# Three reorderings in a fused attention and expert kernel: the readers of the global product, the third products of the first slots, and the last unit's readings

## The chip, the core and the metric

One core of a Trainium2 chip runs the whole program. The core has five engines that run their own instruction streams in order and meet at semaphores: TensorE (PE) for matrix products, VectorE (DVE), ScalarE (ACT), GpSimd (POOL) and SyncE (SP), the last two here also issuing most of the DMAs. TensorE writes its results to PSUM, a small memory from which VectorE and ScalarE copy them to the large one, SBUF. The metric is the time of one execution in microseconds, as the device measures it.

## The reference

A block of attention with local and global tokens feeds a layer of eight experts whose gates are balanced by Sinkhorn iterations. Inputs are eight batches of eight heads with 512 local and 32 global tokens of 64 elements, weights for eight experts with 512 inputs and 1024 hidden values.

```python
# attention: global queries see all keys; local ones a band of 32 to each side and the global keys
s_g   = scale * q_g @ concat(k_g, k_l)^T
out_g = softmax(s_g) @ concat(v_g, v_l)
s_l   = concat(scale * q_l @ k_g^T, where(|i-j| <= 32, scale * q_l @ k_l^T, -1e9))
out_l = softmax(s_l) @ concat(v_g, v_l)
x = concat(out_g, out_l)                      # 4352 tokens of 512
# experts
P = exp(x @ w_gate - max)
for _ in range(8):
    P /= P.sum(1) + 1e-9;  P /= P.sum(0) + 1e-9;  P *= N / E      # N = 4352 tokens, E = 8
out = sum_e P[:, e] * (relu(x @ w1[e]) @ w2[e])
```

## The kernel before

The order on every engine is written out by hand: each engine executes its instructions in the order in which the Python code emits them, and the framework adds the semaphore waits. Buffers come from pools: a tile gets a buffer of its tag when that buffer's last reader is done. The pools that matter here are in PSUM: `ps_mm` (two buffers of tag mm), `ps_sc` (two of sc), `ps_tr` (two of tr), and later `ps_z` (two of z).

**The attention stage** (lines 509 to 626) is a loop over s = 0 to 33. A step s = 4b + hp works on two heads of batch b: scores (`st_B`, tile sc), softmax with VectorE (ms, mx) and ScalarE (Pu), transposes (`st_D1`, `st_D2`), the product with the values (`st_E`, tile po), and the transposes of the next step's keys and queries (`st_A`). Every second step handles four heads of the global queries: `st_G1` in even steps (scores and softmax), `st_G2` and `st_G3` in odd ones. `st_G3` multiplies with the values on TensorE (line 430, ten matmuls into pog, a buffer of tag tr) and then reads pog: a reciprocal on VectorE (line 432, rg), two scalings on VectorE (line 439) and two on ScalarE (line 442), all four into columns of xgn, one tile for four batches. On ScalarE the framework makes the first scaling wait for the two of VectorE. xgn is transposed once after four batches (`st_G4`, at s = 18) and once after the loop.

Between these parts stand pieces of experts 0 and 1, so that TensorE has work while the softmax runs. From s = 5 or 6 a step has four pieces of the first layer (`f1`, tile ph, four matmuls, then a relu on ScalarE for "a" or on VectorE for "v") and from s = 8 two of the second layer (`f2`, tile py, eight matmuls, then a ScalarE copy into yst). All six use the two buffers of `ps_mm` in turn. An odd step ends: `st_E`, `st_G3`, `f2("a")`, `f1("v")`; the next one begins with `f1("a")`, which takes the buffer that the last `f2` held. After the last piece of a tile of yst, SP stores it to yd in device memory.

**The Sinkhorn iterations** follow, with the rest of experts 0 and 1 (`tail`) between them.

**Experts 2 to 7** (lines 691 to 1053) split each product into seven smaller ones (m1 to m7) of half the size in each dimension, by Winograd's form of Strassen's method; sums of the operands are formed by VectorE and GpSimd. A `Slot` is a piece of the first layer for 1024 tokens: pa and pb, pc are PSUM tiles of `ps_mm` and `ps_sc`; m1 goes to pa, ScalarE copies it to pc, m2 adds to pc (then a relu on ScalarE, line 915), m6 and m7 add to pa and are copied (s2, s3), m5 goes to a new pb, `c22` adds s3 to pb on VectorE (line 903). Of the previous slot p, m4 adds to its pa (relu on ScalarE, line 919) and m3 adds to its pb (then a VectorE sum, also line 903). A `Unit` is a piece of the second layer for 256 tokens with its own tile z and products; r1, r2 and r7 are VectorE's readings of z, which scale by P and add to the output. `run_slot` interleaves the slot a, the previous slot p, the unit x that is half done and the unit y that begins. In the first slots there are no units yet; pieces of `tail` fill in (`fill`). After the last slot the last unit x, the last products of p, and the rest of the units follow in a plain form (`plain`, tiles zp and zq).

The order in `run_slot` and at the end is a list of calls:

```python
do(x, "m4", "m5", "r2", "r7")
do(p, "m4")
if x is None:
    do(p, "m3")
do(a, "m2")
if x is not None:
    do(p, "m3")
...
for w in (x.m4, x.m5, x.r2, p.m4, p.m3, x.r7):
    w()
```

Of the kernel before, what the change touches and what calls it, by code (L numbers as in the profile page):

```python
# [23 lines left out]
def kernel(  # L24
# [103 lines left out]
    with ExitStack() as att:  # L128
# [263 lines left out]
        gs = {}  # L392
# [28 lines left out]
        def st_G3(b, g):  # L421
            pgs = gs.pop((b, g))
            va, vb = vab[b % 2]
            vz = vgz[b % 2]
            po = ps_tr.tile([P, 512], FP32, tag="tr", name="pog")
            for t in range(5):
                for par in range(2):
                    r, h0 = slice(HB * par, HB * (par + 1)), 4 * g + 2 * par
                    rhs = vb[:, t, h0 : h0 + 2, :] if t < NJ else vz[:, 3, h0 : h0 + 2, :]
                    nc.tensor.matmul(po[r, 0 : 2 * VW], pgs[:, t, r], rhs, start=(t == 0), stop=(t == 4))  # L430
            rg = att_wk.tile([P, 1], FP32, tag="rg")
            nc.vector.reciprocal(out=rg, in_=po[:, Dh : Dh + 1])
            xg = xgn[b // 4]
            o = slice(W * (b % 4), W * (b % 4 + 1))
            for hh in range(4):
                r = slice(W * hh, W * (hh + 1))
                h = 4 * g + hh
                if hh < 2:
                    nc.vector.tensor_scalar(out=xg[o, Dh * h : Dh * (h + 1)], in0=po[r, VW * (hh % 2) : VW * (hh % 2) + Dh],
                                            scalar1=rg[r, 0:1], scalar2=None, op0=ALU.mult)  # L440
                else:
                    nc.scalar.mul(xg[o, Dh * h : Dh * (h + 1)], po[r, VW * (hh % 2) : VW * (hh % 2) + Dh], rg[r, 0:1])
# [8 lines left out]
        def logits(t0, nt, pool, tag):  # L451
            pl = pool.tile([P, 512], FP32, tag=tag, name="pl")
            for t in range(nt):
                for dk in range(DP):
                    nc.tensor.matmul(pl[:, E * t : E * (t + 1)], xT[:, dk, P * (t0 + t) : P * (t0 + t + 1)],
                                     wg_sb[:, dk, :], start=(dk == 0), stop=(dk == DP - 1))
            nc.vector.tensor_copy(out=lg[:, t0 : t0 + nt, :], in_=pl[:, 0 : E * nt].rearrange("p (t e) -> p t e", e=E))
# [17 lines left out]
        def p_l2(e, m, c, eng, pool=None, tag="mm"):  # L475
            nt = groups[m][1] // P
            if c == 0:
                ysts[(e, m)] = ypool.tile([P, NJ, D], FP32, tag="y", name="yst")
            hT, ys = hTs[(e, m)], ysts[(e, m)]
            py = (pool or ps_mm).tile([P, D], FP32, tag=tag, name="py")  # L480
            for fk in range(FT):
                nc.tensor.matmul(py, hT[:, fk, P * c : P * (c + 1)], wts[e][1][:, fk, :],  # L482
                                 start=(fk == 0), stop=(fk == FT - 1))
            if eng == "a":
                nc.scalar.copy(out=ys[:, c, :], in_=py)  # L485
            else:
                nc.vector.tensor_copy(out=ys[:, c, :], in_=py)
            if c == nt - 1:
                nc.sync.dma_start(out=yd[e][m], in_=ys[:, 0:nt, :])
# [19 lines left out]
        for s in range(NU + 2):  # L509
            b, hp = divmod(s, HP)  # L510
# [53 lines left out]
            def f2(eng):  # L564
                nonlocal n2
                if n2 < len(l2):
                    p_l2(*l2[n2], eng)
                    n2 += 1

            g_odd = s % 2 == 1 and 3 <= s <= NU + 1  # L570
            if g_odd:
                gb, gg = divmod((s - 3) // 2, 2)
# [40 lines left out]
            if g_odd:  # L613
                st_G3(gb, gg)
            f2("a")
            if s >= 6 and (s - 6) % 4 == 0:
                logits(NJ * ((s - 6) // 4), NJ, ps_sc, "sc")
            if s == 8:
# [72 lines left out]
    with tc.tile_pool(name="tpool", bufs=2) as tpool, \  # L691
# [90 lines left out]
        class Unit:  # L782
# [21 lines left out]
            def w(self, i, j):  # L804
                return w2s[self.k][:, HF * i : HF * (i + 1), H2 * j : H2 * (j + 1)]
# [138 lines left out]
        def run_slot(a, jobs=()):  # L944
            p, x = state["slot"], state["unit"]
            y = units.pop(0) if units else None

            def do(who, *what):
                for w in what:
                    if who is not None:  # L950
                        getattr(who, w)()

            def fill(n):
                for _ in range(min(n, len(tail)) if a is not None else 0):
                    tail.pop(0)[1](pool=ps_z, tag="z")

            do(a, "m1")
            some = -(-len(tail) // (HF - a.f)) if tail and a is not None else 0
            if x is None:
                fill(1)  # L960
            if a is not None and p is None:
                fill(1)
                some -= 1
            do(x, "m4", "m5", "r2", "r7")
            do(p, "m4")
            if x is None:
                do(p, "m3")
            do(a, "m2")
            if x is not None:
                do(p, "m3")  # L970
            do(y, "sums", "m1")
            do(a, "m6")
            do(x, "m3", "r1")
            do(a, "m5")
            if y is None:
                fill(some - 1)
            do(y, "m7", "m2", "m6")
            do(a, "m7")
            for j in jobs:
                j()  # L980
            do(a, "c22")
            state["slot"], state["unit"] = a, y
# [30 lines left out]
        for k, (pas, e) in enumerate(stages):  # L1013
# [28 lines left out]
            for (q, f), js in zip(slots, jobs):  # L1042
                if k == 0 and q == 1 and f == 0:
                    hset.append([hpool.tile([P, FT, 512], FP16, tag="hT", name="hs") for _ in range(2)])
                run_slot(Slot(k, q, f, hset[q % 2] if q < NQ else hg), js)
                if q == NQ or f == HF - 1:
                    push(k, q)
        final, units = units, []
        p, x = state["slot"], state["unit"]
        for w in (x.m4, x.m5, x.r2, p.m4, p.m3, x.r7):  # L1050
            w()
        for i, u in enumerate(final):
            plain(u, i == len(final) - 1, (x.m3, x.r1) if i == 0 else ())
# [30 lines left out]
```

## Time and profile before

| what | us |
|---|---|
| median of 3 runs | 1009.54 |
| lowest and highest run | 1008.75, 1011.37 |
| the profiled execution, its time | 1010.12 |
| the profiled execution, its span (first to last instruction) | 1008.4 |
| TensorE busy in the span | 986.0 |
| VectorE, ScalarE, GpSimd busy | 776.8, 632.4, 300.6 |

The span is what the trace covers; the time has 1.7 us more around it. A matmul's start is recorded, its end is modelled, and matmuls overlap: one of 512 columns is shown with about 0.38 us, while its follower starts after less. In a timeline row equal instructions that follow each other are merged ("x8"), the number in brackets is the idle time of the engine before the row with the instruction that ended it, and "out<-in" are the program's tile names. The rows of the profile are shown where the prediction uses them.

### The profile page before, as it was taken

The numbers are of one execution on the slowest core, as the hardware profiler recorded it, in microseconds if no ns is written. First come the engines' busy times: TensorE is split into PE (matmuls) and PEld (weight loads), VectorE is DVE, ScalarE is ACT, GpSimd is POOL, SyncE is SP. The second block draws the span as 40 slices with busy tenths as digits, with TensorE's granted clock in tenths as the row PEclk, the third lists the DMA queues.
The fourth block names the chain that finished last, engine by engine and source line by source line (L and its number), as shares of the span: only waits on it lengthen the run. The fifth ranks groups of instructions, "written<-read, shape, count | busy, mean of one in ns | idle before, by whom it ended". The sixth has DMA issues, their size and how long they took to land.

```text
span 1008.4 us, 22463 instructions
## 1 busy us (share of the span) xinstructions
PE 986.0 (98%) x8868; PEld 640.4 (64%) x8868; DVE 776.8 (77%) x1889; ACT 632.4 (63%) x1342; POOL 300.6 (30%) x366
## 2 busy tenths in 40 slices
PE   7899999999999999999999999999999999999998
PEld 4565555555555545666666666676767676776764
DVE  7776666666664573889999888998889999888885
ACT  5777777777775456765555555557765555555551
POOL 9648888776860022111111111111111111001000
PEclk8999999999999999999999999999999999999999
DMA  9999999999861298555543333466564533223043
GB/s 168 180 155 195 213 241 215 222 191 173 228 180 43 110 224 219 138 140 141 116 116 73 74 74 73 116 177 168 157 147 115 112 85 78 54 72 73 2 105 126
DMA packets 135882, 138.42 MB, mean 137 GB/s; under 512 B 54432, under 2 KB 107872, under 8 KB 133728
## 3 DMA queue, kind: packets, MB, share of 16 engines
q0 software_dynamic: 105696, 87.32, 49.6%
q1 hardware_dynamic: 29520, 49.34, 15.0%
q8 instruction: 69, 1.13, 0.5%
q10 hardware_dynamic: 560, 0.33, 0.1%
q14 instruction: 37, 0.30, 0.1%
HBM read 144.20 MB, written 39.58 MB: 182 GB/s over the span
## 4 chain that ended last, share of the span: by engine, by line
PE 88%; DVE 5%; POOL 2%; DMA 2%; ACT 2%; issue 1%; SPq 0%; ACTq 0%; POOLq 0%; DVEq 0%
PE z L801 30%; PE pa L899 17%; PE ph L468 11%; PE py L482 9%; PE pb L899 9%; PE pc L899 4%; PE ptw L350 1%; PE zp L870 1%; PE sc L331 1%; DVE ms L338 1%; DMA vgz<-vg 1%; DVE xn L389 1%; DMA vg<-in_v_g_dram 1%; PE po L384 1%; ACT yst L485 1%
## 5 line engine op out<-in xcount | busy, mean ns | idle before, releaser
L801 PEld LDWEIGHTS <-hs 128*128 128x128 f16 x2264 | 220.7, 98 | 92.1 <-DVE hs L797 0.9
L801 PE MATMUL z<-w2e,hs 128*128 128x256 f16 x1304 | 195.6, 273 | 0.1
L801 PE MATMUL z<-v,hs 128*128 128x256 f16 x960 | 144.0, 273 | 0.0
L468 PE MATMUL ph<-xT,w1e 128*128 128x512 f16 (+1 forms) x576 | 131.2, 367 | 6.2 <-ACT yst L485 5.9
L482 PE MATMUL py<-w2e,hT 128*128 128x512 f16 x544 | 128.2, 379 | 0.0
L822 ACT COPY z<-z 128x256 f32<-128x256 f32 x98 | 35.0, 357 | 141.8 <-PE z L801 141.8
L899 PEld LDWEIGHTS <-w1e 128*128 128x128 f16 x960 | 87.1, 98 | 51.5 <-issue 1.0
L899 PE MATMUL pa<-t,s 128*128 128x512 f16 x384 | 114.2, 379 | 0.0
L717 POOL DMA_DIRECT2D w1e<-in_moe_w_dram x24 | 17.4, 732 | 300.5 <-PE pa L899 220.5
L341 ACT ACTIVATE Pu<-ms,mx 128x160 f16<-128x160 f32 x256 | 92.4, 424 | 22.9 <-DVE mx L338 20.1
L338 DVE CUSTOM_DVE_ANT_0 ms<-sc,mask 128x160 f32<-128x160 f32 x256 | 69.9, 320 | 43.6 <-PE sc L333 40.6
L835 DVE SCALAR_TENSOR_TENSOR oy<-z,lg,oy 128x512 f32<-128x512 f32 x128 | 95.8, 749 | 8.0 <-ACT oy L840 5.2
L797 DVE TENSOR_TENSOR hs<-hs 128x512 f16<-128x512 f16 x224 | 94.9, 423 | 8.2
L903 DVE CUSTOM_DVE_ANT_0 hx<-pb,s 128x512 f16<-128x512 f32 x96 | 65.9, 686 | 36.8 <-ACT s L933 31.8
L717 POOL DMA_DIRECT2D w2e<-in_moe_w_dram x24 | 19.8, 830 | 243.9 <-PE z L801 214.2
L468 PEld LDWEIGHTS <-w1e 128*128 128x128 f16 x576 | 53.3, 98 | 60.8 <-issue 9.3
L919 ACT ACTIVATE hs<-pa 128x512 f16<-128x512 f32 x96 | 57.2, 596 | 46.8 <-PE pa L899 46.8
L903 DVE CUSTOM_DVE_ANT_0 hs<-pb,s 128x512 f16<-128x512 f32 x96 | 65.8, 686 | 24.5 <-ACT s L933 24.1
L473 DVE TENSOR_SCALAR hT<-ph 128x512 f16<-128x512 f32 x58 | 40.1, 691 | 57.6 <-PE ph L468 57.5
L899 PEld LDWEIGHTS <-s 128*128 128x128 f16 x720 | 65.6, 98 | 29.4 <-issue 1.7
L482 PEld LDWEIGHTS <-hT 128*128 128x128 f16 x544 | 49.8, 98 | 51.9
L471 ACT ACTIVATE hT<-ph 128x512 f16<-128x512 f32 (+1 forms) x86 | 48.0, 558 | 37.4 <-PE ph L468 37.0
(195 smaller groups left out, 1975.1 us busy)
## 6 DMA issues: line engine op xcount, KB each, us to landing
ys<-yd SPq DMA_DIRECT2D x68, 256.0 KB, 3.1
yd<-yst SPq DMA_DIRECT2D x16, 1024.0 KB, 6.5
pw<-in_moe_w_dram POOLq DMA_DIRECT2D x24, 512.0 KB, 9.7
kept<-psum POOLq DMA_DIRECT2D x24, 512.0 KB, 4.9
s<-kept POOLq DMA_DIRECT2D x12, 768.0 KB, 8.8
v<-kept POOLq DMA_DIRECT2D x12, 768.0 KB, 9.1
w1e<-in_moe_w_dram POOLq DMA_DIRECT2D x12, 512.0 KB, 5.3
w2e<-in_moe_w_dram POOLq DMA_DIRECT2D x12, 512.0 KB, 6.6
```

The lines of the kernel that those rows point to most:

```text
L338: nc.vector.tensor_tensor_reduce(out=ms[:, ii, :], in0=sc[:, SW * ii : SW * (ii + 1)], in1=mask[:, mi, :], scale=-scale, scalar=BIG, op0=A ...
L341: nc.scalar.activation(out=d["Pu"][:, i, :], in_=ms[:, ii, :], func=AF.Exp, scale=-1.0, bias=d["mx"][:, i : i + 1])
L468: nc.tensor.matmul(ph[:, 0:n], wts[e][0][:, dk, P * fm : P * (fm + 1)], xT[:, dk, c0 : c0 + n], start=(dk == 0), stop=(dk == DP - 1))
L471: nc.scalar.activation(out=hT[:, fm, 0:n], in_=ph[:, 0:n], func=AF.Relu)
L473: nc.vector.tensor_scalar(out=hT[:, fm, 0:n], in0=ph[:, 0:n], scalar1=0.0, scalar2=None, op0=ALU.max)
L482: nc.tensor.matmul(py, hT[:, fk, P * c : P * (c + 1)], wts[e][1][:, fk, :], start=(fk == 0), stop=(fk == FT - 1))
L797: nc.vector.tensor_tensor(out=o, in0=x, in1=y, op=op)
L801: nc.tensor.matmul(o, lhs[:, fk, :], rhs[:, fk, :], start=(first and fk == 0), stop=(fk == HF - 1), skip_group_check=True)
L835: nc.vector.scalar_tensor_tensor(out=o, in0=z, scalar=p, in1=o, op0=ALU.mult, op1=ALU.add)
L899: nc.tensor.matmul(o, lhs[:, dk, P * f : P * (f + 1)], rhs[:, dk], start=(first and n == 0 and dk == 0), stop=(dk == HD - 1), skip_group_c ...
L903: nc.vector._custom_dve(TENSOR_ADD_SAT, out=self.to(i, j), in0=self.of(ps), in1=self.of(s), s0=BIG, s1=0.0)
L919: nc.scalar.activation(out=self.to(1, 0), in_=self.of(self.pa), func=AF.Relu)
```

## The change

Three places. `st_G3` is cut in two: its matmuls stay, and its readers become `st_G3n`, which the loop calls after the second `f2("a")` of the odd step. In `run_slot`, p.m3 stands after a.m2 in every slot, where slots without a half-done unit x had it before. At the end, r7 is called ahead of p.m4 and p.m3. No instruction of computation is added or removed.

```diff
@@ st_G3
                     nc.tensor.matmul(po[r, 0 : 2 * VW], pgs[:, t, r], rhs, start=(t == 0), stop=(t == 4))
+            gs[(b, g)] = po
+
+        def st_G3n(b, g):
+            po = gs.pop((b, g))
             rg = att_wk.tile([P, 1], FP32, tag="rg")
             nc.vector.reciprocal(out=rg, in_=po[:, Dh : Dh + 1])
@@ the loop over s
             if g_odd:
                 st_G3(gb, gg)
             f2("a")
+            if g_odd:
+                st_G3n(gb, gg)
@@ run_slot
             do(p, "m4")
-            if x is None:
-                do(p, "m3")
             do(a, "m2")
-            if x is not None:
-                do(p, "m3")
+            do(p, "m3")
             do(y, "sums", "m1")
@@ the end
-        for w in (x.m4, x.m5, x.r2, p.m4, p.m3, x.r7):
+        for w in (x.m4, x.m5, x.r2, x.r7, p.m4, p.m3):
             w()
```

Set side by side, the instruction streams of the two programs differ in this: on ScalarE the two scalings of xgn and one copy of yst change places in thirteen steps (s = 9, 11, ... 33); on TensorE two pairs of matmuls change places in four slots (those with a previous slot and no half-done unit); on VectorE the last r7 and the last sum of line 903 change places. SP and POOL issue the same instructions in the same order.

## The prediction
> **What bounds the kernel now.** I read the page first, then the waits of TensorE, then windows by stage, then the timeline around each wait that the change touches.
>
> ```profile
> PE 986.0 (98%) x8868; PEld 640.4 (64%) x8868; DVE 776.8 (77%) x1889; ACT 632.4 (63%) x1342; POOL 300.6 (30%) x366
> PE 88%; DVE 5%; POOL 2%; DMA 2%; ACT 2%; issue 1%; SPq 0%; ACTq 0%; POOLq 0%; DVEq 0%
> PE ph L468 <- ACT yst L485: 5.9, 12, 0.5
> 0.00:60.00 60.00, 48.67 (x862) 31.70 (x863) 46.05 (x207) 41.97 (x104) 49.37 (x79) 0.94 1.41 160
> 60.00:330.00 270.00, 263.71 (x3218) 155.95 (x3217) 167.31 (x639) 196.02 (x451) 182.37 (x191) 1.00 0.97 189
> 395.00:985.00 590.00, 590.00 (x4327) 409.02 (x4326) 514.75 (x929) 355.30 (x714) 57.46 (x81) 1.00 0.44 106
> ```
>
> Columns of the windows: stretch, then PE, PEld, DVE, ACT and POOL busy, granted clock, DMA share, GB/s. TensorE is the bound, 98% busy, and from 395 to 985 us it shows no idle at all. So only time in which TensorE stands still can be won, and the waits view names its largest item: 5.9 us in 12 waits of the first expert layer (ph) on the ScalarE copy yst. All lie in the attention stage, which loses 270.00 - 263.71 = 6.3 us. The first edit is aimed at exactly these waits.
>
> **Edit 1: the readers of the global product go behind the copy.** One odd step of the attention loop, and the even step before it (timeline: start, length, engine, line, tile, count, idle before it and releaser):
>
> ```profile
> 110.50 1.90 PE L482 MATMUL py<-w2e,hT 128*128 128x512 f16 x8
> 112.24 1.89 PE L468 MATMUL ph<-xT,w1e 128*128 128x512 f16 x8
> 112.44 0.58 ACT L485 COPY yst<-py 128x512 f32<-128x512 f32 x1 [0.28 <-PE py L482]
> ...
> 120.72 1.90 PE L482 MATMUL py<-w2e,hT 128*128 128x512 f16 x8
> 122.45 1.03 PE L468 MATMUL ph<-xT,w1e 128*128 128x512 f16 x4
> 123.98 1.02 PE L468 MATMUL ph<-xT,w1e 128*128 128x512 f16 x4 [0.50 <-ACT yst L485]
> 122.04 0.57 DVE L439 TENSOR_SCALAR xgn<-pog,rg 32x64 f16<-32x64 f32 x2
> 122.70 0.62 ACT L442 ACTIVATE xgn<-pog,rg 32x64 f16<-32x64 f32 x2 [0.61 <-PE py L482]
> 123.35 0.58 ACT L485 COPY yst<-py 128x512 f32<-128x512 f32 x1
> ```
>
> In the odd step ScalarE is idle for 0.61 us, held by its two global readings (L442). They start 0.09 after VectorE's two have ended (122.04 + 0.57 = 122.61), take 0.62, and only then comes the copy, 0.73 after py ended (120.72 + 1.90 = 122.62). The next step's first ph needs the PSUM buffer that py occupies (a ring of two, the other held by the ph in between), and stands until 123.98. In the even step the copy starts 0.04 after py's end and the eight ph matmuls run on without a wait.
>
> Matmuls are 0.215 apart ((1.89 - 1.03) / 4), so four of them take 0.86, and the stall measured from start to start is 123.98 - 122.45 - 0.86 = 0.67, not 0.50. The idle column counts from a modelled end, which lies behind the point at which the next matmul could have begun.
>
> [...]
>
> After the edit ScalarE is free when py ends, so the copy should run 122.66 to 123.24. With the 0.05 that TensorE needs to see it (123.35 + 0.58 = 123.93, start at 123.98) ph may start at 123.29; its natural time is 122.45 + 0.86 = 123.31. The margin is thin, 0.02, but the even step has the same one (112.44 + 0.58 + 0.05 = 113.07 against 112.24 + 0.86 = 113.10) and shows no wait. So the whole 0.67 goes.
>
> ```profile
> 81.83 1.02 PE L468 MATMUL ph<-xT,w1e 128*128 128x512 f16 x4 [0.50 <-ACT yst L485]
> 311.20 1.03 PE L468 MATMUL ph<-xT,w1e 128*128 128x512 f16 x4
> 312.59 1.02 PE L468 MATMUL ph<-xT,w1e 128*128 128x512 f16 x4 [0.36 <-ACT yst L485]
> ```
>
> These are the first and the last of the twelve. Eleven have an idle of 0.50, the last 0.36, which is 312.59 - 311.20 - 0.86 = 0.53 by starts. Sum: 11 x 0.67 + 0.53 = **7.9 us**. The edit moves thirteen places; the thirteenth (s = 33) has no wait in the view and is put at nothing.
>
> What is late next: the two readings now run at about 123.24 to 123.87 (0.62 as before). Behind them on ScalarE stands the relu of the next ph, which cannot be asked for before 123.31 + 1.03 = 124.34; that ph matmul group is the cover, and without it the readings would cost 0.62 a step. VectorE's order does not change: the copy between is ScalarE's. Nobody needs the readings soon: pog's buffer is next wanted by a transpose of the following step, xgn only by two late transposes. No DMA is added. The ones that hang on a copy (yd on SP) are issued earlier by the stall.
>
> Bounds of edit 1: not above the 7.9, since four matmuls cannot issue faster; below, half of it, if the thin margin breaks to 0.3 a step.
>
> **Edit 2: the third product in slots without units.** Four slots near 375, 380, 385 and 392 us. Per slot TensorE issues pairs of 0.43: p.m4 (pa<-t,w1e), p.m3 (pb<-xT,s), a.m2 (pc), a.m6, a.m5 (new pb).
>
> ```profile
> 375.21 0.59 PE L899 MATMUL pa<-t,w1e 128*128 128x512 f16 x2
> 375.78 0.59 PE L899 MATMUL pb<-xT,s 128*128 128x512 f16 x2
> 377.15 0.59 PE L899 MATMUL pb<-xT,w1e 128*128 128x512 f16 x2
> 375.04 0.69 DVE L903 CUSTOM_DVE_ANT_0 hx<-pb,s 128x512 f16<-128x512 f32 x1 [2.03 <-issue]
> 376.41 0.69 DVE L903 CUSTOM_DVE_ANT_0 hx<-pb,s 128x512 f16<-128x512 f32 x1 [0.68 <-PE pb L899]
> 375.03 0.57 ACT L911 COPY pc<-pa 128x512 f32<-128x512 f32 x1
> 375.85 0.60 ACT L919 ACTIVATE hs<-pa 128x512 f16<-128x512 f32 x1
> 376.84 0.60 ACT L915 ACTIVATE hs<-pc 128x512 f16<-128x512 f32 x1 [0.40 <-PE pc L899]
> 377.33 0.58 ACT L924 COPY s<-pa 128x512 f32<-128x512 f32 x1
> ...
> 379.76 0.59 PE L899 MATMUL pa<-t,w1e 128*128 128x512 f16 x2
> 380.45 0.59 PE L899 MATMUL pb<-xT,s 128*128 128x512 f16 x2
> 381.82 0.59 PE L899 MATMUL pb<-xT,w1e 128*128 128x512 f16 x2
> ...
> 391.70 0.59 PE L899 MATMUL pa<-t,w1e 128*128 128x512 f16 x2
> 392.43 0.59 PE L899 MATMUL pb<-xT,s 128*128 128x512 f16 x2
> 391.71 0.57 ACT L911 COPY pc<-pa 128x512 f32<-128x512 f32 x1
> ```
>
> p.m3 waits for VectorE's sum c22 (375.04 + 0.69 = 375.73) and starts 0.14, 0.26, 0.26 and 0.30 after its natural time (375.78 against 375.64, 380.45 against 380.19, the third taken like the second, 392.43 against 392.13). a.m5 loses 0.08 more in the first three (377.15 against 375.78 + 1.29 = 377.07): it takes the buffer that p.m3's own sum frees (376.41 + 0.69 = 377.10). With a.m2 ahead, p.m3 comes 0.43 later and c22 is done. The pool hands out the buffer that is freed first, which now is a.m2's: the waits of the changed program put a.m5 behind a.m2's relu on ScalarE. In slot 1 that relu follows p.m4's at 375.85 by 0.49 (as 377.33 follows 376.84), ends at 376.94, and a.m5 starts near 376.98: 0.17 won. Slots 2 and 3, with p.m4's relu 0.64 into the slot likewise, win 0.30 each. In slot 4 a.m2 meets the copy of pc (391.71 + 0.57 + 0.05 = 392.33, 0.20 late), so 0.10 is left. Sum **0.87 us**. Bounds: 1.20 won if every one of these stalls goes; 0.53 lost if a.m5 still waits for p.m3's later sum (0.29 + 0.17 + 0.17 lost, 0.10 won). I take the value near the first, as the program's waits say.
>
> **Edit 3: the last unit's readings ahead of the last sum.** The chain of waits near the end, and its TensorE row:
>
> ```profile
> 989.46 0.69 DVE hs L903
> 990.15 0.67 DVE oy L835
> 990.86 0.61 PE z L801 x4
> 991.50 0.76 DVE oy L835
> 992.30 11.39 PE zp L870 x56
> ...
> 989.26 1.46 PE L870 MATMUL zp<-w2e,hs 128*128 128x512 f16 x6
> ```
>
> x.m3 (990.86) waits for r7 (ends 990.82), which stands behind the sum (989.46). Without that wait it would start after its six matmuls, 989.26 + 6 x 0.215 = 990.55. With r7 first, from 989.46 for about 0.76, it is done at 990.22 and the sum at 990.91. x.m3 starts at 990.55, r1 0.64 later at 991.19, behind the finished sum, and the second zp follows r1 as before: **0.31 us** won, nothing at worst. The sum's product is read only in that zp's last matmuls. r7's output store enters SP's queue earlier, in the same place.
>
> **Sum.** 7.9 + 0.87 + 0.31 = 9.1 us. The stages follow each other on TensorE, so the terms add. The profiled execution took 1010.12: 1010.12 - 9.1 = **1001.0 us**. It lies 0.6 above the median of the runs, which would give 1000.5.
>
> **Rivals.**
> A. *Only the visible idle goes*, through the thin margin: 5.9 won, edits 2 and 3 nothing: 1004.2. For: 0.02 of margin. Against: the even step.
> B. *The transfers take over.* Edit 1 asks for the same bytes in 7.9 / 270 = 2.9% less time while the DMA share is 0.97; TensorE would then wait for loads and keep only edits 2 and 3: 1008.9. Against: 0.97 is no ceiling, since the first 60 us show 1.41, and the queue that issues the loads itself waits for TensorE:
>
> ```profile
> POOL vb L174 <- PE pog L430: 13.7, 3, 6.8
> ```
>
> C. *Slower: the granted clock gives way* where TensorE gets denser, from 81 us on. Over 986 us busy each 0.01 costs 9.9 us, so it outweighs the gain once the mean falls by 0.009; at 0.02 less the time is 1001.0 + 19.7 = 1020.7. For: the stage gains 2.9% in density. Against: the window 395 to 985 is fully dense at 1.00.
>
> [...]
>
> D. *Edit 2 turns into its lower bound*: 1010.12 - 7.9 - 0.31 + 0.53 = 1002.4.
>
> **How the numbers follow.** Forecast 0.74 (999.6 to 1002.5), D 0.07, A 0.10, B 0.06, C 0.03. A measurement tells about 0.3% (3 us) from no change. Faster: forecast, D and A, 0.91; within: B, 0.06; slower: C, 0.03. The range reaches up to A's 1004.2, and down to the lowest run shown (1008.75) less the 9.1, less another 0.9: 0.3 up to edit 2's upper bound and the 0.6 by which the profiled run stood above the median: 998.8.
>
> **What would show it.** Edit 1 right: the row of ph on yst is gone from TensorE's waits, ph runs x8 across odd steps, the attention stage is 7.9 shorter. Edit 2: a.m2 before p.m3 with no gap above 0.05 in slots 1 to 3. Edit 3: x.m3 directly behind six zp. Wrong: a new wait of TensorE on a DMA (B), a clock under 0.99 (C), ph still late on yst (A).

## The result, and the profile after

| what | before | after |
|---|---|---|
| median of 6 runs, us | 1009.09 | 1000.87 |
| lowest and highest run | 1006.71, 1011.37 | 998.91, 1003.41 |
| the profiled execution: time, span | 1010.12, 1008.4 | 1000.96, 999.2 |
| mean granted clock | 0.996 | 0.995 |

The changed kernel is faster: the ratio of the times is 0.992 with a 95% interval of 0.990 to 0.9941. By the medians of six runs it gains 8.2 us. The prediction said 1001.0 for the profiled execution, from a range of 998.8 to 1004.2.

In the changed program the lines behind the new function stand four to six lower: ph is L472, py L486, the copy yst L489, the two scalings on ScalarE L446; the products of a slot L905, the sum c22 L909, the relus L921 and L925; the products of a unit L807, its readings L841, zp L876. Up to L430 nothing moves. First the page of the profile (busy time by engine, then the chain that ended last), a row of TensorE's waits, and the windows of the attention loop from 60 us on and of the expert stage (stretch; PE, PEld, DVE, ACT and POOL busy; granted clock, DMA share, GB/s):

```profile
PE 984.4 (99%) x8868; PEld 641.4 (64%) x8868; DVE 777.1 (78%) x1889; ACT 631.9 (63%) x1342; POOL 300.6 (30%) x366
PE 96%; DVE 2%; ACT 1%; issue 0%; DVEq 0%; ACTq 0%
PE tgx L360 <- DVE pw L352: 3.0, 3, 1.4
60.00:322.10 262.10, 260.71 (x3215) 155.72 (x3214) 166.80 (x637) 195.01 (x449) 181.56 (x190) 1.00 0.98 194
386.00:976.00 590.00, 590.00 (x4327) 409.00 (x4326) 515.28 (x930) 355.22 (x714) 57.46 (x81) 1.00 0.45 107
```

The row of ph waiting for yst, the largest of before, is gone. The chain that ended last is TensorE's for 96% of the span, against 88%. The attention window has 1.4 us without TensorE busy (262.10 - 260.71), against 6.3. The clock stands at 1.00 from 60 us on, and the DMA share is 0.98 at 194 GB/s: TensorE has no wait for a transfer in that stretch. GpSimd does wait for loads: its sums of the weights (psum) stood 40.7 us for them here and 30.6 before. The row of waits shown has grown from 2.1 to 3.0, though, and one of the three is 1.4 long. It comes back below.

To see which stage gave what, the execution is cut at starts of TensorE that both programs have: the first py, the first pa of the slots, the first z of the units. The rows by tile give the first start of each (count, ns of one at least, median and most, then first and last start in us); before, then after:

```profile
L482 PE MATMUL py<-w2e,hT x544: 376/379/390, 62.7 to 390.2; 128*128 128x512 f16 x182
L899 PE MATMUL pa<-xT,w1e x240: 219/379/379, 366.1 to 981.3; 128*128 128x512 f16 x96, 128*128 128x128 f16 x24
```
```profile
L486 PE MATMUL py<-w2e,hT x544: 376/379/390, 61.8 to 381.4; 128*128 128x512 f16 x182
L905 PE MATMUL pa<-xT,w1e x240: 219/379/379, 358.1 to 972.5; 128*128 128x512 f16 x96, 128*128 128x128 f16 x24
```

With the two decimals of the timeline:

| stretch of the profiled execution, us | before | after | difference | predicted |
|---|---|---|---|---|
| start of the span to the first py | 62.69 | 61.84 | -0.85 | 0 |
| first py to first pa (edit 1) | 303.46 | 296.26 | -7.20 | -7.9 |
| first pa to first z, the four slots (edit 2) | 27.15 | 26.32 | -0.83 | -0.87 |
| first z to first zp | 595.97 | 595.97 | 0.00 | 0 |
| first zp to the end (edit 3) | 19.09 | 18.79 | -0.30 | -0.31 |

The sum, -9.18, is within 0.1 of the prediction's -9.1. It is the sum of two misses that cancel: the attention stretch gave 0.7 less than was forecast, and the start-up, which no edit touches, was 0.85 shorter.

**Edit 1 in the timeline.** An odd step of after (start, length, engine, line, tile, count, idle before it and releaser):

```profile
118.25 1.90 PE L486 MATMUL py<-w2e,hT 128*128 128x512 f16 x8
119.99 1.89 PE L472 MATMUL ph<-xT,w1e 128*128 128x512 f16 x8
119.58 0.57 DVE L443 TENSOR_SCALAR xgn<-pog,rg 32x64 f16<-32x64 f32 x2
120.19 0.58 ACT L489 COPY yst<-py 128x512 f32<-128x512 f32 x1 [0.56 <-PE py L486]
120.80 0.62 ACT L446 ACTIVATE xgn<-pog,rg 32x64 f16<-32x64 f32 x2
121.92 0.60 ACT L475 ACTIVATE hT<-ph 128x512 f16<-128x512 f32 x1 [0.49 <-PE ph L472]
```

ph runs as x8 across the step. py ends at 118.25 + 1.90 = 120.15, the copy starts 0.04 later and ends at 120.77; the fifth ph is due at 119.99 + 0.86 = 120.85. The 0.05 between a copy's end and the start of the matmul that waits for it fits, with 0.03 to spare: the thin margin held in all twelve places. The two readings (120.80 to 121.42) delay nothing that TensorE waits for, and the relu behind them waits for ph, not for them.

**Edit 2.** The first of the four slots:

```profile
367.17 0.59 PE L905 MATMUL pa<-t,w1e 128*128 128x512 f16 x2
367.61 0.59 PE L905 MATMUL pc<-xT,w1e 128*128 128x512 f16 x2
368.04 0.59 PE L905 MATMUL pb<-xT,s 128*128 128x512 f16 x2
368.46 0.59 PE L905 MATMUL pa<-t,s 128*128 128x512 f16 x2
368.93 0.59 PE L905 MATMUL pb<-xT,w1e 128*128 128x512 f16 x2
368.29 0.59 ACT L921 ACTIVATE hs<-pc 128x512 f16<-128x512 f32 x1
368.67 0.69 DVE L909 CUSTOM_DVE_ANT_0 hx<-pb,s 128x512 f16<-128x512 f32 x1 [0.99 <-PE pb L905]
```

The pairs follow at 0.43, save the last: a.m5 comes 0.47 after a.m6. It starts 0.05 after a.m2's relu ends (368.29 + 0.59 = 368.88), and 0.43 before p.m3's own sum ends (368.67 + 0.69 = 369.36). So it cannot be waiting for p.m3's buffer; it takes a.m2's, as the prediction read from the program's waits.

**Edit 3.** The end of the chain:

```profile
980.38 1.46 PE L876 MATMUL zp<-w2e,hs 128*128 128x512 f16 x6
981.67 0.60 PE L807 MATMUL z<-w2e,hs 128*128 128x256 f16 x4
982.11 0.59 PE L876 MATMUL zp<-w2e,hs 128*128 128x512 f16 x2
983.12 1.24 PE L876 MATMUL zp<-w2e,hs 128*128 128x512 f16 x5 [0.41 <-DVE oy L841]
979.81 1.53 DVE L841 SCALAR_TENSOR_TENSOR oy<-z,lg,oy 128x512 f32<-128x512 f32 x2
981.26 0.68 DVE L909 CUSTOM_DVE_ANT_0 hs<-pb,s 128x512 f16<-128x512 f32 x1
982.31 0.75 DVE L841 SCALAR_TENSOR_TENSOR oy<-z,lg,oy 128x512 f32<-128x512 f32 x1 [0.37 <-PE z L807]
```

The readings now run as x2 ahead of the sum, x.m3 stands directly behind its six zp (980.38 + 6 x 0.215 = 981.67), and the second zp still waits for r1 for 0.41.

### The profile page after: what moved, and what is told of

Same layout as the page of the kernel before. It is cut to its first block, busy times and chain, and to the rows that moved or that the text cites. A ratio compares the mean times of both kernels' runs of the same rounds, so it can differ in the third digit from the quotient of the medians.

```text
span 999.2 us, 22452 instructions
## 1 busy us (share of the span) xinstructions
PE 984.4 (99%) x8868; PEld 641.4 (64%) x8868; DVE 777.1 (78%) x1889; ACT 631.9 (63%) x1342; POOL 300.6 (30%) x366
## 4 chain that ended last, share of the span: by engine, by line
PE 96%; DVE 2%; ACT 1%; issue 0%; DVEq 0%; ACTq 0%
PE z L807 30%; PE pa L905 18%; PE py L486 12%; PE ph L472 12%; PE pb L905 9%; PE pc L905 4%; PE po L384 2%; PE ptw L350 1%; PE zp L876 1%; PE sc L331 1%; PE pk L299 1%; DVE ms L338 1%; PE tgx L360 1%; PE pq L299 1%; ACT Pu L341 1%; PE sg L403 0%
## 5 line engine op out<-in xcount | busy, mean ns | idle before, releaser
L807 PEld LDWEIGHTS <-hs 128*128 128x128 f16 x2264 | 220.7, 98 | 91.8 <-DVE hs L803 1.0
L807 PE MATMUL z<-w2e,hs 128*128 128x256 f16 x1304 | 195.6, 273 | 0.0
L807 PE MATMUL z<-v,hs 128*128 128x256 f16 x960 | 144.0, 273 | 0.0
L472 PE MATMUL ph<-xT,w1e 128*128 128x512 f16 (+1 forms) x576 | 129.3, 367 | 0.3 <-ACT xT L368 0.3
L486 PE MATMUL py<-w2e,hT 128*128 128x512 f16 x544 | 128.2, 379 | 0.0
L905 PEld LDWEIGHTS <-w1e 128*128 128x128 f16 x960 | 87.1, 98 | 51.6 <-issue 1.0
L905 PE MATMUL pa<-t,s 128*128 128x512 f16 x384 | 114.2, 379 | 0.0
L841 DVE SCALAR_TENSOR_TENSOR oy<-z,lg,oy 128x512 f32<-128x512 f32 x128 | 95.9, 749 | 7.6 <-ACT oy L846 5.1
L909 DVE CUSTOM_DVE_ANT_0 hx<-pb,s 128x512 f16<-128x512 f32 x96 | 65.9, 687 | 36.4 <-ACT s L939 30.3
L472 PEld LDWEIGHTS <-w1e 128*128 128x128 f16 x576 | 53.4, 98 | 52.9
L925 ACT ACTIVATE hs<-pa 128x512 f16<-128x512 f32 x96 | 57.2, 596 | 47.0 <-PE pa L905 47.0
L909 DVE CUSTOM_DVE_ANT_0 hs<-pb,s 128x512 f16<-128x512 f32 x96 | 65.9, 686 | 24.1 <-ACT s L939 23.6
L905 PEld LDWEIGHTS <-s 128*128 128x128 f16 x720 | 65.6, 98 | 28.5 <-issue 0.3
L486 PEld LDWEIGHTS <-hT 128*128 128x128 f16 x544 | 49.8, 98 | 51.9
L120 POOL TENSOR_TENSOR psum<-pw 128x512 f16<-128x512 f16 x48 | 55.1, 1184 | 40.7 <-DMA pw<-in_moe_w_dram 40.7
```

Of the source, the lines that this page charges most:

```text
L120: nc.gpsimd.tensor_tensor(out=o, in0=x, in1=y, op=op)
L472: nc.tensor.matmul(ph[:, 0:n], wts[e][0][:, dk, P * fm : P * (fm + 1)], xT[:, dk, c0 : c0 + n], start=(dk == 0), stop=(dk == DP - 1))
L807: nc.tensor.matmul(o, lhs[:, fk, :], rhs[:, fk, :], start=(first and fk == 0), stop=(fk == HF - 1), skip_group_check=True)
L841: nc.vector.scalar_tensor_tensor(out=o, in0=z, scalar=p, in1=o, op0=ALU.mult, op1=ALU.add)
L905: nc.tensor.matmul(o, lhs[:, dk, P * f : P * (f + 1)], rhs[:, dk], start=(first and n == 0 and dk == 0), stop=(dk == HD - 1), skip_group_c ...
L909: nc.vector._custom_dve(TENSOR_ADD_SAT, out=self.to(i, j), in0=self.of(ps), in1=self.of(s), s0=BIG, s1=0.0)
```

## The experiments

The stretches of the table above can be taken from every run, so each edit can be read in its own stretch even where the whole time is too coarse. Medians of before are those of the same session.

**1. Edit 1 alone**, put on the kernel before; the order in the slots and at the end stays old.

> The kernel before with edit 1 alone (the global readers behind the copy). Theory (the copy's place on ScalarE is the whole cause): the twelve waits of ph on yst are gone, the first pa of experts 2 to 7 starts some 7.9 us earlier than the 366.1 of before, slots 1 to 4 keep their gaps ahead of pb, the time is about 7.9 us under the kernel before. Rival (the visible idle alone goes): 5.9 us. Rival (the stall only moves to another wait): under 2 us.

Measured: 1000.72 against 1008.72, ratio 0.9914 (0.989 to 0.9938). The wait of ph on yst is gone, the attention stretch is 296.27, the slots keep 27.15 and the end 19.10. So edit 1 carries the gain in time: 8.0 of it by the medians.

**2. The other way to take the same wait away.** The order of before, with all four scalings on VectorE:

```diff
-                if hh < 2:
+                if hh < 4:
```

> The kernel before, nothing moved, but all four scalings of the global product run on VectorE, so none stands ahead of the copy on ScalarE. Theory (queue order on ScalarE): the same 7.9 us as edit 1 alone, as VectorE has room for two more scalings of 0.28 before its next relu. Rival (it is the later place in the step that wins, or the wait for VectorE that the copy inherits): the waits of ph stay and the time stays near that of before, or VectorE's relu becomes late and half the gain is lost.

Measured: 1002.59, ratio 0.9929 (0.9907 to 0.9952); attention 296.03, and no wait of ph on yst. By the medians that is 6.1 gained, against 8.0 in run 1; by the stretch it is 7.4 against 7.2. The first py stands at 63.23 us here and at 60.32 in run 1, which makes the profiled execution longer ahead of any edit. Nothing else was moved: what had delayed py's copy was ScalarE's place in line and not, for example, the arrival of py.

**3. Half of the stall put back**: in the changed kernel one of ScalarE's two scalings goes ahead of the copy again.

```diff
             if g_odd:
                 st_G3(gb, gg)
+                st_G3n(gb, gg, (0, 1, 2))
             f2("a")
             if g_odd:
-                st_G3n(gb, gg)
+                st_G3n(gb, gg, (3,))
```

> The changed kernel, but one of the two ScalarE scalings (with the reciprocal and VectorE's two) stands ahead of the copy again. Theory: the copy then starts 0.31 us earlier than before the change, so a stall of 0.36 us by starts is left in eleven steps and 0.20 in the last: 4.2 us of the 7.9 come back, time about 1005. Rival (what counts is whether the copy waits for VectorE at all): the full 7.9 us come back, 1008.8. Rival (a reading of 0.3 fits into the cover): 0 comes back.

Measured: 1003.66, ratio 0.9946 (0.9926 to 0.9966). The row of waits, and one step of the timeline:

```profile
PE ph L474 <- ACT yst L491: 2.0, 11, 0.2
```
```profile
120.42 1.03 PE L474 MATMUL ph<-xT,w1e 128*128 128x512 f16 x4
121.64 1.02 PE L474 MATMUL ph<-xT,w1e 128*128 128x512 f16 x4 [0.18 <-ACT yst L491]
120.67 0.30 ACT L448 ACTIVATE xgn<-pog,rg 32x64 f16<-32x64 f32 x1 [0.60 <-PE py L488]
121.00 0.58 ACT L491 COPY yst<-py 128x512 f32<-128x512 f32 x1
```

The stall is 121.64 - 120.42 - 0.86 = 0.36 by starts where the idle column has 0.18. Over the stage the starts give 4.0, the idle column 2.0. The attention stretch is 298.91, 2.65 longer than in after: more than the idle column could make and less than the starts make, so something else took 1.3 less in this run. Matmul by matmul, the starts of the two traces show what: ph loses 3.99 and tgx, the transposes that wait for VectorE's copies Pl and pw, wins 1.34. Most of that, 1.55, is one step: near 278 us in after the copy Pl takes 2.32 us and TensorE stands for it, while here it takes 0.62 and TensorE does not wait. Another step, near 177 us here, loses 0.34. Why the copy is long is the subject of runs 7 to 10.

**4. Edit 2 alone**, on the kernel before.

> The kernel before with edit 2 alone (the third product later in four slots). Theory: first pa unchanged near 366.1, and the slots between it and the first z are 0.87 us shorter, 26.3 instead of 27.15; a.m5 waits for a.m2's relu and hardly stalls. Rival (a.m5 still waits for the now later sum): 0.53 us longer, 27.7. The attention waits of ph on yst stay at 5.9.

Measured in one run: the slots take 26.32, the attention 303.24 with all twelve waits (5.9), the end 19.14. The time of this run, 1011.29, lies 2.6 above the median of before: 0.83 us can't be seen in one time, but its own stretch is the 26.32 of after again.

**5. Edit 2 without its buffer.** In the changed kernel, slots 1 to 3 give pc and pb the buffers of the slot before, as the old order did, so that only the order is new:

```diff
-                self.pc = ps_sc.tile([P, 512], FP32, tag="sc", name="pc")
+                self.pc = self.prev.pc if self.prev else ps_sc.tile([P, 512], FP32, tag="sc", name="pc")
...
-                self.pb = ps_sc.tile([P, 512], FP32, tag="sc", name="pb")
+                self.pb = self.prev.pb if self.prev else ps_sc.tile([P, 512], FP32, tag="sc", name="pb")
...
+            a.prev = p if x is None and y is None else None
```

> The changed kernel, but in slots 1 to 3 a.m5 writes into the PSUM buffer of p.pb again, and pc into that of p.pc, as before the change. Theory (edit 2 wins because a.m5 gets a.m2's buffer and so waits for a short relu): a.m5 now stalls for the later sum, slots 1 to 3 end 0.63 us later than before the change and slot 4 still wins 0.10, so the stretch from the first pa to the first z is 27.7 us (before 27.15, changed 26.32). Rival (the order alone wins, whatever the buffer): 26.3 us.

```profile
371.55 0.59 PE L905 MATMUL pb<-xT,s 128*128 128x512 f16 x2
371.98 0.59 PE L905 MATMUL pa<-t,s 128*128 128x512 f16 x2
372.92 0.59 PE L905 MATMUL pb<-xT,w1e 128*128 128x512 f16 x2 [0.35 <-DVE hx L909]
372.18 0.69 DVE L909 CUSTOM_DVE_ANT_0 hx<-pb,s 128x512 f16<-128x512 f32 x1 [0.98 <-PE pb L905]
```

The slots take 27.73, which is 0.58 longer than before where the change is 0.83 shorter. a.m5 now waits for p.m3's sum (372.18 + 0.69 = 372.87). This is rival D's mechanism, near its predicted size of 0.53. The new order by itself would have cost time; it wins because the pool then hands a.m5 the other buffer.

**6. Edit 3 alone**, on the kernel before.

> The kernel before with edit 3 alone (r7 ahead of the last sum). Theory: x.m3 starts right behind six zp matmuls, and the stretch from the first zp to the end of the span is 0.31 us shorter, 18.8 instead of 19.1; everything ahead as before. Rival (r1 is then late behind the sum): 19.1 or longer.

```profile
988.74 1.46 PE L870 MATMUL zp<-w2e,hs 128*128 128x512 f16 x6
990.04 0.60 PE L801 MATMUL z<-w2e,hs 128*128 128x256 f16 x4
```

x.m3 follows its six zp after 1.30, and the end takes 18.81 (19.09 before). Measured in one run, 1009.33. Over all profiled executions the end takes 18.66 to 18.83 with the new order and 19.09 to 19.14 with the old one.

**What the missing 0.7 is.** All twelve stalls of edit 1 are gone by starts, 7.85 us, yet the stretch gave 7.20. TensorE issues the same matmuls in the same order in this stretch of both programs, so their starts can be set side by side: ph wins 7.82 in all and tgx loses 0.60, which makes the 7.2. The 0.60 is 1.12 lost in one step, near 278 us, less 0.1 to 0.2 won in each of three others. After:

```profile
274.75 1.89 PE L486 MATMUL py<-w2e,hT 128*128 128x512 f16 x8
274.95 2.32 POOL L120 TENSOR_TENSOR psum<-pw 128x512 f16<-128x512 f16 x2
275.06 2.32 DVE L347 COPY Pl<-Pu 128x256 f16<-128x256 f16 x1
277.30 0.68 DVE L352 COPY pw<-ptw 128x1024 f16<-128x1024 f16 x1
277.36 1.15 POOL L120 TENSOR_TENSOR psum<-psum,pw 128x512 f16<-128x512 f16 x1
278.03 0.38 PE L360 MATMUL tgx<-identity,xn 128*128 128x128 f16 x4 [1.39 <-DVE pw L352]
```

The same step of before:

```profile
282.75 1.89 PE L482 MATMUL py<-w2e,hT 128*128 128x512 f16 x8
283.02 1.15 POOL L120 TENSOR_TENSOR psum<-pw,psum 128x512 f16<-128x512 f16 x1
283.06 1.20 DVE L347 COPY Pl<-Pu 128x256 f16<-128x256 f16 x1
284.91 0.38 PE L360 MATMUL tgx<-identity,xn 128*128 128x128 f16 x4 [0.27 <-DVE pw L352]
```

VectorE's copy Pl (the share of the global keys, 128 x 256 in SBUF) takes 0.22 us in about half of the steps of after. Here it ends when GpSimd's sums of the weights end: 0.10 behind them in after (274.95 + 2.32 = 277.27 against 277.38), 0.09 in before. The copy pw, which tgx needs, stands behind it on VectorE. TensorE starts tgx 3.28 after py in after and 2.16 in before, so this one step lost 1.12 us more. Of the eleven copies of after that take over 0.3 us (from 65 us on), ten end 0.08 to 0.10 behind a sum. Which copy falls on which sum changes from run to run; that it follows from when GpSimd's loads arrive is likely, since the sums wait for them and not equally long in each execution (40.7 us in after and 38.6 in run 1, which have the same attention order; 33.1 in run 10 and 39.1 in run 12, which are the same kernel), but was not tested. Two theories: the hold comes with this form of the copy, or with any VectorE operation of this kind beside GpSimd.

**7. Another form of the same copy**, a maximum of the operand with itself:

```diff
-            nc.vector.tensor_copy(out=d["Pl"], in_=d["Pu"][:, :, KW:SW])
+            nc.vector.tensor_tensor(out=d["Pl"], in0=d["Pu"][:, :, KW:SW], in1=d["Pu"][:, :, KW:SW], op=ALU.max)
```

> The changed kernel, but the copy Pl<-Pu on VectorE is written as max(x, x) of two equal inputs, the same values. Theory (the long copies of up to 2.3 us are ones that start while a GpSimd sum runs and are locked out of memory until it ends, which the plain copy's form brings about): no instruction of that line above 0.5 us, no wait of TensorE for them in the steps from s = 8, the stretch from the first py to the first pa near 295.0 us instead of 296.26, time about 1 us under the changed kernel. Rival (any VectorE instruction on these tiles is held up beside GpSimd): long ones stay, stretch 296 or more.

Measured: 1001.09, ratio 0.9926 (0.9904 to 0.9948), attention 296.64. The theory, the form, fell, and the rival's 296 or more came true:

```profile
226.05 2.25 DVE L347 TENSOR_TENSOR Pl<-Pu 128x256 f16<-128x256 f16 x1
225.80 2.34 POOL L120 TENSOR_TENSOR psum<-pw 128x512 f16<-128x512 f16 x2
```

It is held as long as the plain copy, until the second sum ends (228.14; the maximum ends at 228.30): 2.25 us here, 2.32 in after. What in the hardware makes either wait for the sums, no run here shows.

**8. The copy on ScalarE, in the same place.**

```diff
-            nc.vector.tensor_copy(out=d["Pl"], in_=d["Pu"][:, :, KW:SW])
+            nc.scalar.copy(out=d["Pl"], in_=d["Pu"][:, :, KW:SW])
```

> The changed kernel, but the copy Pl<-Pu runs on ScalarE. Theory (lock between VectorE's copy and GpSimd): no long copy is left, stretch from the first py to the first pa near 295.0 us, if ScalarE's queue takes 0.35 us more a step without making ph wait for yst. Rival (the added copy makes yst late): the wait of ph on yst comes back with 0.1 to 0.35 us in some steps and the stretch is 297 or more.

Measured: 1003.15, ratio 0.9941 (0.9919 to 0.9962), attention 298.15. The first row of TensorE's waits:

```profile
PE tgx L364 <- ACT Pl L347: 4.6, 5, 1.7
```

The copy takes 387 to 395 ns, so none is held on ScalarE; but there it stands behind the exponentials of the step, and TensorE waits for it 4.6 us instead. Neither theory nor rival had that: ph does not wait for yst, it is tgx that waits for the copy itself.

**9. No sums on GpSimd.** The sums of the weights of experts 2 to 7 are left out and zeros are stored in their place.

```diff
-        for o, x, y, op in ops:
-            nc.gpsimd.tensor_tensor(out=o, in0=x, in1=y, op=op)
+        if n == 0:
+            nc.gpsimd.memset(work["s"], 0.0)
```

> The changed kernel without GpSimd's sums of the weights (the four per step are left out and zeros are stored for experts 2 to 7); its DMAs stay. Theory (a running GpSimd sum holds VectorE's copy up): from s = 9 on no Pl<-Pu takes more than 0.36 us, and the stretch from the first py to the first pa is near 295.0. Rival (something else, such as DMA writes, holds the copy): long ones of 0.6 us and more stay.

Measured in one run: attention 294.62, every copy Pl behind 65 us at its short length of about 0.22. With the sums gone the holds are gone, and the stretch is 1.6 shorter than in after. So the ten copies that end with a sum are held by it. The eleventh, 1.00 us at 83.28, has no sum beside it, but GpSimd's issues of loads (L171, L174); in this run no copy met such an issue, so what held that one stays open.

**10. The copy on ScalarE early**: at the very beginning of the next step, ahead of its exponentials.

```diff
-        def st_D1(n):
+        def st_D0(n):
...
-            nc.vector.tensor_copy(out=d["Pl"], in_=d["Pu"][:, :, KW:SW])
+            nc.scalar.copy(out=d["Pl"], in_=d["Pu"][:, :, KW:SW])
+
+        def st_D1(n):
...
+            if 1 <= s <= NU:
+                st_D0(s - 1)
             f1("a")
```

> The changed kernel, but the copy Pl<-Pu runs on ScalarE at the very start of the step, ahead of the first relu, where ScalarE is idle for 1.1 us. Theory (VectorE's copy is held up by GpSimd's running sum, and the copy on ScalarE was late only by its place): no long copy, no wait of TensorE on Pl from s = 8 on, stretch from the first py to the first pa 294.7 to 295.2 us against 296.26, time about 1 us under the changed kernel. Rival (ScalarE has no room there): the relu or yst becomes late and the stretch is 296 or more.

Measured: 999.04 (997.94 to 1001.43), ratio 0.9896 (0.9879 to 0.9912), attention 294.59. The step at 275 us:

```profile
274.76 0.41 ACT L347 COPY Pl<-Pu 128x256 f16<-128x256 f16 x1
274.38 2.26 POOL L120 TENSOR_TENSOR psum<-pw 128x512 f16<-128x512 f16 x2 [1.54 <-DMA pw<-in_moe_w_dram]
276.78 1.89 PE L489 MATMUL py<-w2e,hT 128*128 128x512 f16 x8
278.51 0.39 PE L363 MATMUL tgx<-identity,xn 128*128 128x128 f16 x4
```

The copy runs beside a sum and takes 0.41, and in all other steps from 65 us on 0.40 to 0.41; tgx follows py after 1.73, eight matmuls at 0.216, with no gap.

**11 and 12. The changed kernel and this one once more**, side by side.

> The changed kernel once more, beside share_early on the same chip. Theory: stretch from the first py to the first pa between 294.7 (no copy held up at a bad moment) and 296.3, as the holds fall differently in each run; ratio to before near 0.992.

> The version with the copy on ScalarE at the start of the step, beside the changed kernel. Theory: stretch again 294.6 us, since no copy can be held up; the median 0.2 to 1.7 us under the changed kernel, which the rounds may not separate. Rival: the first run's 294.59 was luck, and it is 295.5 or more now.

Measured: 999.96 (997.92 to 1003.52, ratio 0.9894, 0.9867 to 0.9922) for the change, 1000.35 (996.07 to 1003.93, ratio 0.9901, 0.9871 to 0.9932) for the early copy. By time they can't be told apart; the early copy's median is even 0.4 above. By stretch they can: 295.40 (longest copy 1.21 us) against 294.59, the latter the same to the hundredth as in run 10. In the two profiled executions what outweighs the 0.8 us is the start-up, which differs by 6.5. The first py of the two repeats:

```profile
L486 PE MATMUL py<-w2e,hT x544: 376/379/390, 65.2 to 383.9; 128*128 128x512 f16 x182
```
```profile
L489 PE MATMUL py<-w2e,hT x544: 376/379/390, 58.7 to 376.6; 128*128 128x512 f16 x182
```

Over all profiled executions it lies between 58.7 and 65.7 us. Part of it is one load: TensorE's wait for vgz, 2.3 us in the first of these and absent from the waits of the second. The rest was not taken apart.

## Why the prediction was right

**Edit 1** was right in its mechanism and in the counting of starts. The twelve stalls were 7.85 by starts, of the predicted 7.9, and none over 0.05 is left; runs 1 and 2 show that ScalarE's order was the cause, run 3 that half of the delay leaves half of the sum by starts (4.0 of 7.85). What the stretch gains is less. Three executions with the old order have attention stretches of 303.46, 303.24 and 304.03, mean 303.58; four with the new one and no other edit in that stage have 296.26, 296.27, 295.94 and 295.40, mean 295.97. The difference of the means, 7.6, is what the edit is worth here; the 0.3 that is missing lies within the spread of the four, 0.9, in which the copies that VectorE makes late, held by GpSimd, are the part that the runs could name (in the profiled pair the transposes behind them took back 0.60). No term of the prediction held them: they can be seen in the trace of before, and its paragraph on what is late next did not ask whether they would fall differently once TensorE ran earlier. The step that was mis-sized is the net of edit 1, by 0.3 in the mean and 0.7 in the profiled execution.

**Rival A** (only the visible 5.9) is out: the margin of 0.02 held, and the stage gave more than 5.9. The margin was as thin as said, 0.03 in the step shown. **Rival B** is out: the DMA share rose from 0.97 to 0.98 in the stage and no new wait of TensorE for a transfer appeared. **Rival C** is out: the clock is 1.00 from 60 us on in both, 0.995 against 0.996 over the span.

**Edit 2**: 0.83 against 0.87. The steps held one by one in slot 1, even to the releaser; in the other three a.m2 is 0.03, 0.06 and 0.20 late, the 0.20 being the copy of pc in the fourth slot, which the prediction had taken off. **Rival D** did not occur, and its 1002.4 lies inside the forecast's own range, so only the stretch could tell the two apart. Run 5 made it occur, at 0.58 for the 0.53: the choice between the bounds hung on which buffer the pool hands out, and reading that from the program's waits was the right evidence.

**Edit 3**: 0.30 against 0.31, alone (run 6, 0.28) as in the change.

**The sum** was nearer than its parts deserve. The 0.85 of the start-up is chance, and without it the profiled execution would have been 1001.8: still within the forecast's own range of 999.6 to 1002.5.

## What to carry to other kernels

Where an in-order engine both frees a ring buffer of PSUM and serves readers that nobody waits for, the copy that frees the buffer goes first; price the stall by the starts of TensorE, since the idle column showed 5.9 of 7.85 us here and 2.0 of 4.0 in run 3. When two products change places, look up which buffer the pool now hands out: here the new order gained 0.83 us with the pool's choice and lost 0.58 with the old buffers kept. Judge small edits by the stretch that holds them, between starts that both programs share: 0.3 us was plain there while whole times vary by more than 4. A stretch has its own spread, though: the attention's was 0.9 over four executions of the same code.

## What was not expected of the hardware

A small copy between SBUF tiles on VectorE, 0.22 us alone, took up to 2.32 us, because it ended only after two GpSimd sums in a row had (1.22 and 1.21 us). By the trace it was overtaken: the second sum began at 276.07, when the copy had been waiting for a microsecond. GpSimd's times are not sharp, for the first sum is shown to end only at 276.17 (274.95 + 1.22), 0.10 after the second began; but the copy's own 2.32 us is about twice what one sum takes. In three of the traces the longest hold spans two sums: 2.32 us in after, 1.91 in run 5 and 2.25 in run 7. VectorE's copies out of PSUM kept their 0.68 to 0.69 us beside the same sums (L352 at 277.30, with a sum from 277.36), and ScalarE's copy out of SBUF its 0.40 to 0.41.
